# A chunked linear attention and two expert layers on one core: state products in four quadrants, weights converted in whole chunks, the second block's first product in halves, fewer loads up front

## The chip, the cores and the metric

The kernel runs on one core of a Trainium2 chip. The metric is the device time of one execution in microseconds, as the median of several runs; a separate profiled execution gives the trace. TensorE is called PE here, VectorE DVE, ScalarE ACT, GpSimd POOL, and SP is the engine whose queue issues the transfers.

## The reference

Attention with a decaying state runs over batch 4, 8 heads, 768 positions and head size 48. Its output, 3072 tokens of 384, goes through two expert layers, 384 to 2048 to 384 each.

```python
for t in range(S):
    kt, vt, rt = (k[:, :, t], v[:, :, t], r[:, :, t])
    cur = np.einsum('bhd,bhe->bhde', u[None] * kt, vt)
    y[:, :, t] = np.einsum('bhd,bhde->bhe', rt, state + cur)
    state = w[None, :, :, None] * state + np.einsum('bhd,bhe->bhde', kt, vt)
...
h = x @ w_in                                  # first layer
sp = np.where(h > 20.0, h, np.log1p(np.exp(np.minimum(h, 20.0))))
x = (h * np.tanh(sp)) @ w_out
...
h = np.maximum(x @ w_in, 0.0)                 # second layer
out = (h * h) @ w_out
```

The expert weights arrive as 64-bit floats and are turned into 32-bit ones on the core.

## The kernel before

**Work.** The positions are cut in 6 chunks of 128, so there are 24 attention units n = 4c + b (chunk c, batch b). A unit makes the scores of all heads (`scores`, tiles sc, L402), fills and masks a matrix A (`fill` on ACT, `select` on DVE), and sums the unit's y of two kinds of products: old state times r, one 112x112 product for each pair of heads (L433, only for c > 0), and A times v, one product for each head into 48 or 64 columns of the array (L442). Then it makes the new state's addend s (`s_pe`, L460), copies y to the stage tile yst (`y_out`, L473), and updates the state S. A pair of heads lies in rows 0 to 47 and 64 to 111.

The experts run over 12 blocks of 512 tokens, named in `BLOCKS` as (layer, chunk): (1,0), (1,1), (2,0), (2,1), (1,2) and so on. A block has 16 steps j, each over 128 of the 2048 hidden columns: `up` writes h (three 128x512 products), `act1` or `act2` makes g of it on ACT and DVE, and `down1` or `down2`, four steps later, adds to three or four accumulators acc. h has three buffers: up has two and flex one. The first two blocks are called full: their products are plain 32-bit ones on the tile wf (L575, L651). All other blocks split each operand into a high and a low half of a faster type and make three products for one, in `mm3` (L560 to L562).

**Weights.** Each step's weights are two halves of 384 columns. `conv_half` loads one half (raw, 64-bit), and turns it into wf with one ACT and three DVE instructions. The first layer's 16 chunks are converted while block 0 runs, the second's while blocks 1 and 2 run (`make_w2`, which also splits them in halves); both go to DRAM (wd1, wd2) and come back later.

**The spread.** After the four units of a chunk, six small transfers (`spread`) move the rows of the fourth pair of heads in yst between partitions, and `split_x` makes the expert input x of it.

**What sets the order.** Every instruction group is an item with an engine, an estimated time, and a due number. `Plan.order` plays all engines through once and writes the groups out in the order in which they would run; each engine then runs its own list strictly in that order, and SP's list is the queue of transfers. A ring of n buffers lets a tile start when the users of the n-th tile before it are done. `gates` hold a transfer back until a given `up` has been placed.

Of the kernel before, what the change touches and what calls it, by code (L numbers as in the profile page):

```python
# [33 lines left out]
class Tl:  # L34


    def __init__(self, ring, shape, dtype, name, ap=None):
        self.ring, self.shape, self.dtype, self.name, self.ap = ring, list(shape), dtype, name, ap
        self.users, self.writer, self.readers = [], None, []

    def get(self):
        if self.ap is None:
# [20 lines left out]
class Plan:  # L63
# [8 lines left out]
    def add(self, eng, dur, due, fn, r=(), w=(), deps=()):  # L72

        it = dict(n=len(self.items), eng=eng, dur=dur, due=due, fn=fn, deps=list(deps), after=[], ready=0.0)
# [16 lines left out]
    def order(self, rings):  # L91
        items = self.items
        for ring in rings:
            for k, t in enumerate(ring.tiles):
                if k >= ring.bufs:
                    t.users[0]["deps"] += ring.tiles[k - ring.bufs].users
                if k:
                    t.users[0]["after"].append(ring.tiles[k - 1].users[0])
# [14 lines left out]
        while events:  # L113
# [5 lines left out]
            for e, q in queue.items():  # L119
# [8 lines left out]
                else:  # L128
                    it["end"] = free[e] = now + it["dur"]
# [24 lines left out]
def rwkv_moe_kernel(ctx: ExitStack, tc: tile.TileContext, good, rk, nat, wT, wrow, ub, cst, w1, w2, out):  # L154
# [19 lines left out]
    for p, tag, bufs in (  # L174
        (w_p, "hi", NF + 1), (w_p, "lo", NF),
        (conv_p, "raw", 4), (conv_p, "wf", 2),
        (st_p, "stage", 1),
        (in_p, "r", 2), (in_p, "k", 2), (in_p, "nat", 2), (in_p, "v", 2),
        (a_p, "dg", 2), (a_p, "A", 2),
        (f_p, "e", 3), (f_p, "r", 2), (f_p, "ghi", 3), (f_p, "glo", 3), (f_p, "o", 3),  # L180
# [19 lines left out]
    def dma(o, i):  # L200
        nc.sync.dma_start(out=o, in_=i)
# [8 lines left out]
    one = const.tile([128, 1], F32, name="one")  # L210
    mask = cst_sb[:, 0:128].bitcast(I32)
# [5 lines left out]
    Sb = [fixed(const.tile([HP, NP, HP], F32, name=f"S{b}"), f"S{b}") for b in range(B)]  # L217
# [36 lines left out]
    for b in range(B):  # L254
        add("POOL", 0.5, -198 + b, lambda b=b: nc.gpsimd.memset(Sb[b].ap, 0.0), w=[Sb[b]])
# [16 lines left out]
    W = {}  # L272
    wd = {(2, x): fixed(dram_p.tile([NF, 128, 768], F32, name=f"wd2{x}"), f"wd2{x}") for x in ("hi", "lo")}
    wd1 = fixed(dram_p.tile([NF, 128, 768], F32, name="wd1"), "wd1")
    wdj = {}

    def conv_half(layer, j, half, f, fcol, due, raw_ring):
# [3 lines left out]
        raw = R[raw_ring].new([128, DM, 2], U32, f"raw{layer}_{j}_{half}")  # L281
        src = (w1, w2)[layer - 1][j, half]

        def load():
            dma(raw.get().rearrange("p d t -> p (d t)"), src.bitcast(U32))

        def fu():
            return f[:, fcol:fcol + DM].bitcast(U32)

        def s0():  # L290
            nc.scalar.activation(f[:, fcol:fcol + DM], raw[:, :, 1].bitcast(F32), AF.Copy, scale=HSC)
# [13 lines left out]
        add("ACT", 0.54, due - 1.5, s0, r=[raw], w=[f])  # L305
        add("DVE", 0.32, due - 1, s2, r=[f], w=[f])
        add("DVE", 0.53, due - 0.8, s3, r=[raw, f], w=[f])
        add("DVE", 0.53, due - 0.6, s4, r=[raw, f], w=[f])

    def split_w(layer, j, f, fcol, due):  # L310

        half = fcol // DM
        if half == 0 or (layer, j) not in W:
            W[layer, j] = [R[x].new([128, 768], F32R, f"w{x}{layer}_{j}") for x in ("hi", "lo")]
        hi, lo = W[layer, j]
        return hi, lo

    def split_hi(f, src, hi, dst):
        nc.scalar.activation(hi.get()[:, dst:dst + DM], f[:, src:src + DM], AF.Copy)

    def split_lo(f, src, hi, lo, dst):
        nc.vector.tensor_tensor(
            lo.get()[:, dst:dst + DM], f[:, src:src + DM], f32v(hi[:, dst:dst + DM]), ALU.subtract
        )

    def store_w(layer, j, due):
        for x, t in zip(("hi", "lo"), W[layer, j]):
            d = wdj[layer, j, x] = fixed(wd[layer, x].ap[j], f"wd{layer}{x}{j}")
            add("SP", 0.393, due, lambda d=d, t=t: dma(d.ap, f32v(t.ap)), r=[t], w=[d])

    def load_w(layer, j, due):
        W[layer, j] = [R[x].new([128, 768], F32R, f"w{x}{layer}_{j}r") for x in ("hi", "lo")]
        for x, t in zip(("hi", "lo"), W[layer, j]):
            d = wdj[layer, j, x]
# [8 lines left out]
    def load_unit(n, due):  # L343
        c, b = units[n]
        early = 2 <= n < B
        u = U[n] = {}
        shapes = ((HP, NP, C), (HP, NP, C), (128, 2, H, D), (128, H, D))
        for x, shape, src, mb in zip(
            ("r", "k", "nat", "v"), shapes, (rk[n, :, 0], rk[n, :, 1], nat[n, :, 0:2], nat[n, :, 2]),
            (0.229, 0.229, 0.393, 0.197),  # L350
        ):
            t = u[x] = R["hi" if early else x].new(shape, F32, f"{x}{n}")
# [4 lines left out]
    def rk_scale(n, x, due):  # L357
        t = U[n][x]
        add("DVE", 0.69, due, lambda: nc.vector.tensor_tensor(t.ap, t.ap, E, ALU.mult), r=[t, T_E], w=[t])
# [31 lines left out]
    def scores(n, due):  # L391
# [4 lines left out]
        def f():  # L396
            for e in range(2):
                ps[e].get()
            for p in range(NP):
                for e in range(2):  # L400
                    q = slice(64 * e, 64 * e + D)
                    nc.tensor.matmul(ps[e][:, p, :], u["k"][q, p, :], u["r"][q, p, :], start=True, stop=True)  # L402

        add("PE", 1.0, due, f, r=[u["k"], u["r"]], w=ps)
# [18 lines left out]

    def y_pe(n, due):
        u = U[n]
        c, b = units[n]
        ps = u["y"] = R["at"].new([128, NP, 128], F32, f"y{n}")

        def f():
            o = ps.get()  # L430
# [6 lines left out]
            v = u["v"].ap.rearrange("q h d -> q (h d)")  # L437
            for p in range(NP):
                for e in range(2):

                    h, m = 2 * p + e, 64 if not c and e == 0 else D
                    nc.tensor.matmul(  # L442
                        o[64 * e:64 * e + m, p, :], v[:, h * D:h * D + m], u["A", e][:, p, :],
# [3 lines left out]
        add("PE", 2.0 if c else 1.1, due, f, r=[u["r"], u["v"], u["A", 0], u["A", 1], Sb[b]], w=[ps])  # L447

    def s_pe(n, due):
# [3 lines left out]
        ps = u["s"] = R["at"].new([128, NP, 128], F32, f"s{n}")  # L453

        def f():
            o = ps.get()
            for p in range(NP):
                for e in range(2):
                    h = 2 * p + e
                    nc.tensor.matmul(  # L460
                        o[64 * e:64 * e + D, p, 0:D], u["nat"][:, 1, h, :], u["v"][:, h, :], start=True, stop=True
                    )

        add("PE", 0.6, due, f, r=[u["nat"], u["v"]], w=[ps])

    def y_out(n, due):
# [5 lines left out]
        def f():  # L472
            nc.scalar.activation(ys.get()[0:HP, :, b * C:(b + 1) * C], y[0:HP], AF.Copy)  # L473

        add("ACT", 0.6, due, f, r=[y], w=[ys])

    def state(n, due):
# [3 lines left out]
        ps = U[n]["s"]  # L481
        s = Sb[b]
        if c:
            add(
                "DVE", 0.6, due - 0.3,
# [547 lines left out]
```

## Time and profile before

| | us |
|---|---|
| median of 3 runs | 962.73 (961.9 to 962.97) |
| the profiled execution | 960.92 |
| its span in the trace | 959.0 |
| PE busy | 927.3 |
| DVE busy | 621.3 |
| ACT busy | 614.0 |

The span is the stretch that the trace covers; the execution's time is 1.9 us longer. Busy times overlap, since the engines run side by side. PE's first expert product starts 40.73 us after the span's start and its last product 951.77 us after it.

### The profile page before, as it was taken

To read this page: it belongs to the slowest core of one execution; us is meant where nothing else is said; L and a number is where in the kernel's file an instruction comes from. 1 tells how busy PE (TensorE), PEld (TensorE's weight loads), DVE (VectorE), ACT (ScalarE), POOL (GpSimd) and SP (SyncE) were. 2 spreads that over 40 slices of the span, in tenths; PEclk is the share of its full clock that TensorE was granted. 3 is DMA by queue.
4 is the path that set the end of the run, shared out by engine and by line. 5 is a ranking of instruction groups with operands and counts; after the bars stand their busy time and mean duration, and the time that the engine had idled before them with its cause. 6 is when DMAs were issued, how large, how long until landed. Compare 5 with 4: busy or idle time off the path is not lost.

```text
span 959.0 us, 13135 instructions
## 1 busy us (share of the span) xinstructions
PE 927.3 (97%) x4808; PEld 730.5 (76%) x4808; DVE 621.3 (65%) x1107; ACT 614.0 (64%) x1135; POOL 1.9 (0%) x9
## 2 busy tenths in 40 slices
PE   4699999999999999999999999999999999999997
PEld 3445444446988998888888889898888888899996
DVE  6899988999844566877988532363778877211211
ACT  3676567777755676787867655476767777544442
POOL 0000000000000000000000000000000000000000
PEclk9799999999999999999999999999999999999999
DMA  9894143578623443201366312243100065200001
GB/s 278 284 346 142 66 141 107 179 247 276 219 85 102 135 133 112 84 1 53 105 214 224 109 45 93 76 136 116 59 1 10 20 211 189 92 1 1 33 1 37
DMA packets 48106, 114.18 MB, mean 119 GB/s; under 512 B 5985, under 2 KB 12386, under 8 KB 48034
## 3 DMA queue, kind: packets, MB, share of 16 engines
q1 hardware_dynamic: 48034, 113.26, 35.9%
q8 instruction: 40, 0.66, 0.3%
q14 instruction: 32, 0.26, 0.1%
HBM read 88.47 MB, written 23.59 MB: 117 GB/s over the span
## 4 chain that ended last, share of the span: by engine, by line
PE 92%; DMA 4%; DVE 2%; issue 0%; SPq 0%; ACT 0%; DVEq 0%
PE h L560 12%; PE h L562 12%; PE h L561 11%; PE acc L651 8%; PE h L575 7%; PE acc L689 7%; PE acc L691 7%; PE acc L690 7%; PE acc L560 5%; PE acc L562 5%; PE acc L561 5%; PE sc L402 2%; PE y L442 2%; PE y L433 2%; DMA raw<-in_w_dram 1%; DMA r<-in_rk_dram 1%
## 5 line engine op out<-in xcount | busy, mean ns | idle before, releaser
L628 DVE TENSOR_TENSOR glo<-g,ghi 128x512 fp32r<-128x512 f32 x96 | 66.1, 689 | 150.4 <-ACT ghi L623 150.3
L636 ACT ACTIVATE e<-h 128x512 f32<-128x512 f32 x96 | 57.4, 598 | 116.4 <-PE h L562 116.2
L607 ACT ACTIVATE e<-h 128x512 f32<-128x512 f32 x96 | 56.9, 593 | 65.1 <-PE h L562 35.1
L623 ACT ACTIVATE ghi<-e 128x512 fp32r<-128x512 f32 x96 | 60.5, 630 | 59.1 <-PE acc L690 57.1
L575 PE MATMUL h<-x,wf 128*128 128x512 f32 x192 | 89.5, 605 | 4.9 <-ACT x L542 4.0
L651 PE MATMUL acc<-g,wf 128*128 128x512 f32 x192 | 88.1, 595 | 1.6 <-DVE g L604 1.6
L612 DVE TENSOR_TENSOR e<-e,r 128x512 f32<-128x512 f32 x96 | 66.1, 689 | 27.3 <-ACT r L611 27.0
L560 PE MATMUL acc<-ghi,whi 128*128 128x512 f32 x192 | 76.8, 400 | 0.0
L560 PE MATMUL h<-xh_a,whi 128*128 128x512 f32 x192 | 76.3, 397 | 0.0
L562 PE MATMUL h<-xh_a,wlo 128*128 128x512 f32 x192 | 75.6, 394 | 0.0
L562 PE MATMUL acc<-ghi,wlo 128*128 128x512 f32 x192 | 75.3, 392 | 0.0
L561 PE MATMUL h<-xl_a,whi 128*128 128x512 f32 x192 | 74.9, 390 | 0.0
L561 PE MATMUL acc<-glo,whi 128*128 128x512 f32 x192 | 74.8, 389 | 0.0
L575 PEld LDWEIGHTS h<-x,wf 128*128 128x128 f32 x192 | 36.6, 193 | 49.9 <-issue 39.9
L608 ACT ACTIVATE e<-e,one 128x512 f32<-128x512 f32 x96 | 69.4, 723 | 2.9
L651 PEld LDWEIGHTS acc<-g,wf 128*128 128x128 f32 x192 | 36.0, 190 | 44.7 <-issue 40.4
L601 DVE SCALAR_TENSOR_TENSOR r<-e,r 128x512 f32<-128x512 f32 x96 | 66.4, 692 | 3.2
L610 ACT ACTIVATE r<-e 128x512 f32<-128x512 f32 x96 | 59.7, 622 | 12.8 <-DVE e L598 12.5
L387 ACT ACTIVATE A<-cst_sb,dg 128x128 f32<-128x128 f32 x192 | 59.4, 388 | 6.2 <-DVE dg L372 6.2
L637 ACT ACTIVATE g<-e 128x512 f32<-128x512 f32 x96 | 60.6, 632 | 3.6 <-DVE glo L628 0.8
L611 ACT ACTIVATE r<-r 128x512 f32<-128x512 f32 x96 | 60.6, 632 | 2.9
L740 DVE TENSOR_TENSOR wlo<-wk,whi 128x768 fp32r<-128x768 f32 x32 | 30.6, 957 | 46.9 <-ACT g L637 21.1
(273 smaller groups left out, 2094.5 us busy)
## 6 DMA issues: line engine op xcount, KB each, us to landing
raw<-in_w_dram SPq DMA_DIRECT2D x64, 384.0 KB, 5.6
wk<-wd SPq DMA_DIRECT2D x32, 384.0 KB, 4.2
nat<-in_nat_dram SPq DMA_DIRECT2D x24, 384.0 KB, 4.1
wd<-wf SPq DMA_DIRECT2D x16, 384.0 KB, 3.1
wd2hi<-whi SPq DMA_DIRECT2D x16, 384.0 KB, 2.6
wd2lo<-wlo SPq DMA_DIRECT2D x16, 384.0 KB, 2.7
r<-in_rk_dram SPq DMA_DIRECT2D x24, 224.0 KB, 3.0
k<-in_rk_dram SPq DMA_DIRECT2D x24, 224.0 KB, 3.6
```

Of the source, the lines that this page charges most:

```text
L560: nc.tensor.matmul(o, wh, xh, start=first, stop=False, skip_group_check=True)
L561: nc.tensor.matmul(o, wh, xl, start=False, stop=False, skip_group_check=True)
L562: nc.tensor.matmul(o, wl, xh, start=False, stop=last, skip_group_check=True)
L575: nc.tensor.matmul(o, w[:, k * 128:(k + 1) * 128], xs[k][0].ap, start=(k == 0), stop=(k == 2))
L601: nc.vector.scalar_tensor_tensor(r.ap, e.ap, 2.0, r.ap, ALU.subtract, ALU.mult)
L608: add("ACT", 0.73, d + 0.2, lambda: nc.scalar.activation(e.ap, e.ap, AF.Square, bias=one), r=[e, T_one], w=[e])
L612: add("DVE", 0.69, d + 1, lambda: nc.vector.tensor_tensor(e.ap, e.ap, r.ap, ALU.mult), r=[e, r], w=[e])
L628: lambda: nc.vector.tensor_tensor(lo.get(), g.ap, f32v(hi.ap), ALU.subtract), r=[g, hi], w=[lo],
L651: nc.tensor.matmul(o, w[:, sl], hi.ap, start=(j == 0), stop=(j == NF - 1), skip_group_check=True)
L689: nc.tensor.matmul(o, hi[:, sl], wh[:, 384:768], start=(j == 0), stop=False, skip_group_check=True)
L690: nc.tensor.matmul(o, hi[:, sl], wl[:, 384:768], start=False, stop=False, skip_group_check=True)
L691: nc.tensor.matmul(o, lo[:, sl], wh[:, 384:768], start=False, stop=(j == NF - 1), skip_group_check=True)
```

## The change

1. The old-state products go from one 112x112 product for a pair of heads to one product for each head, in a 64x64 quarter of the array (`side` and `place` say which; pairs 1 and 2 swap their column halves). y of pairs 0 and 3 is in one PSUM bank and y of pairs 1 and 2 in another; s is written into the same two banks behind y. The state tile has 48 columns for each pair and not 112, and the updates of S and the copies of y go by bank.
2. A weight chunk is loaded and converted whole (768 columns). Two whole raw buffers take the place of four half ones.
3. Block 1's `up` uses halves: `FULL_UP` is (0,) and `FULL_DOWN` is (0, 1). The 384 up columns of each first-layer chunk are split (tiles wu), and x of chunk 1 too.
4. The first-layer chunks from the seventh on are loaded behind the first spread; r and k of a unit come in one transfer, and so do the two parts of nat with v. Half of the first spread is issued by ACT.
5. There are four output buffers o and not three.

```diff
-        (w_p, "hi", NF + 1), (w_p, "lo", NF),
-        (conv_p, "raw", 4), (conv_p, "wf", 2),
+        (w_p, "wa", NF // 2), (w_p, "wb", NF // 2),
+        (conv_p, "raw", 2), (conv_p, "wf", 2),
...
-        (f_p, "e", 3), (f_p, "r", 2), (f_p, "ghi", 3), (f_p, "glo", 3), (f_p, "o", 3),
+        (f_p, "e", 3), (f_p, "r", 2), (f_p, "ghi", 3), (f_p, "glo", 3), (f_p, "o", 4),
...
+    FULL_UP, FULL_DOWN = (0,), (0, 1)
...
-        raw = R[raw_ring].new([128, DM, 2], U32, f"raw{layer}_{j}_{half}")
+        raw = R[raw_ring].new([128, 768, 2], U32, f"raw{layer}_{j}")
...
-        it = add("SP", 0.393, due - 8 if layer == 2 else -175 + 10 * j, load, w=[raw])
+        it = add("SP", 0.786, load_due, load, w=[raw])
         if layer == 2:
-            gates.append((it, int(due - 8)))
+            gates.append((it, int(load_due)))
+        elif j >= 6:
+            gates.append((it, -1))
...
+    def side(p, e):
+        return 64 * (e ^ (p in (1, 2)))
+
+    def place(p):
+        return (0, 0) if p == 0 else (0, 1) if p == 3 else (1, p - 1)
...
             if c:
-                for p in range(NP):
+                for p, e in ((0, 0), (0, 1), (1, 1), (1, 0), (3, 0), (3, 1), (2, 1), (2, 0)):
+                    x, y = slice(64 * e, 64 * e + D), side(p, e)
+                    m = D if y else 64
                     nc.tensor.matmul(
-                        o[0:HP, p, :], Sb[b].ap[:, p, :], u["r"][:, p, :],
-                        start=(p == 0), stop=False, skip_group_check=True,
+                        out_y(p, y, m), Sb[b].ap[x, p * D:p * D + m], u["rk"][x, 0, p, :],
+                        start=(p < 2), stop=False, skip_group_check=True,
                     )
...
-        ps = u["s"] = R["at"].new([128, NP, 128], F32, f"s{n}")
+        ps = u["y"]
...
-        k_scale(n, t + d)
         for e in range(2):
             select(n, e, t + d)
         y_pe(n, t + 2 * d)
+        k_scale(n, t + d)
         s_pe(n, t + 2 * d)
...
-        def f():
+        def f(e):
+            eng = nc.scalar if c == 0 and e else nc.sync
             for k in range(3):
-                dma(ys[48:64, k, :], ys[16 * k:16 * k + 16, 3, :])
-                dma(ys[112:128, k, :], ys[64 + 16 * k:80 + 16 * k, 3, :])
+                dma(ys[64 * e + 48:64 * e + 64, k, :], ys[64 * e + 16 * k:64 * e + 16 * k + 16, 3, :], eng)
...
-        if blk in FULL:
+        if blk in FULL_UP:
             w = WF[j]
...
-        wh, wl = W[layer, j]
+        wh, wl = WU[j] if blk in FULL_DOWN else W[layer, j]
...
+            if 1 not in FULL_UP:
+                if j % 2 == 0:
+                    tile2 = R["wb"].new([128, 2, 2, 384], F32R, f"wu{j}")
+                WU[j] = [tile2.part(lambda ap, a=j % 2, x=x: ap[:, a, x]) for x in range(2)]
+                split_w(WF[j], slice(0, 384), *WU[j], NF + j - 3)
```

On PE the first place is unit 8, in block 2. Before, its y and s stand together (x4 and x8 are that many products, each of two passes):

```order
L562 MATMUL h_2186<-xh_b_1265,wlo_11_1907 128x512
L433 MATMUL y_2201<-r_1605,S_101 112x128 x4
L442 MATMUL y_2201<-A_0_1799,v_1620 48x128
L442 MATMUL y_2201<-A_1_1890,v_1620 48x128
...
L460 MATMUL s_2218<-v_1620,nat_1613 48x48 x8
L689 MATMUL acc_2_1862<-whi_8_1651,ghi_2112 128x384
```

Of the change (y_0 and y_1 are the two banks, and s has the name of y; L496 are the state products, L506 those of A, L525 those of s):

```order
L642 MATMUL h_2033<-xh_b_1172,w_11_1793 128x512
L496 MATMUL y_0_2048<-rk_1518,S_101 64x128
L496 MATMUL y_0_2048<-rk_1518,S_101 48x128
L496 MATMUL y_1_2051<-rk_1518,S_101 64x128
L496 MATMUL y_1_2051<-rk_1518,S_101 48x128
...
L506 MATMUL y_0_2048<-A_1_1846,nat_1522 48x128
L769 MATMUL acc_2_1737<-w_8_1628,ghi_1963 128x384
...
L771 MATMUL acc_2_1749<-w_8_1628,glo_1969 128x384
L525 MATMUL y_0_2048<-nat_1522 64x48
```

Four state products have become eight, and s has moved behind the twelve products of a `down2`. So it is in all of units 4 to 19; before, s stood right behind y in 11 of these 16.

The second place is ACT's list ahead of the first expert input x. Before, from the third unit's copy on:

```order
L473 ACTIVATE yst_292<-y_350 112x4x128
L387 ACTIVATE A_0_385<-cst_sb,dg_362 128x128 x4
L387 ACTIVATE A_1_393<-cst_sb,dg_362 128x128 x4
L497 ACTIVATE S_103<-s_364 48x4x48 x2
L291 ACTIVATE wf_0_192<-raw_0_1_150 128x384
L291 ACTIVATE wf_4_416<-raw_4_0_210 128x384
L291 ACTIVATE wf_1_243<-raw_1_1_162 128x384
L291 ACTIVATE wf_5_431<-raw_5_0_216 128x384
L473 ACTIVATE yst_292<-y_407 112x4x128
```

Of the change:

```order
L539 ACTIVATE yst_248<-y_1_322 112x2x128
L565 ACTIVATE S_103<-y_0_322 112x2x48
L565 ACTIVATE S_103<-y_1_322 112x96
L328 ACTIVATE wf_2_320<-raw_3_162 128x768
L328 ACTIVATE wf_4_373<-raw_4_164 128x768
L328 ACTIVATE wf_4_373<-raw_5_166 128x768
L539 ACTIVATE yst_248<-y_0_362 112x2x128
L539 ACTIVATE yst_248<-y_1_365 112x2x128
L219 DMA yst_248<-yst_248 16x512 x3
```

The copy of the fourth unit's y, on which the spread hangs, stands behind the conversion of the sixth weight chunk (raw_5) here, and behind the first half of that chunk before.

The third place is SP's queue around the first spread. Before, raw halves 6 to 8 went ahead of it, and then unit 4's r and k followed soon:

```order
L201 DMA raw_7_1_239<-in_w_dram 128x768
L201 DMA raw_8_0_398<-in_w_dram 128x768
L201 DMA yst_292<-yst_292 16x512 x6
L201 DMA raw_8_1_445<-in_w_dram 128x768
L201 DMA raw_9_0_450<-in_w_dram 128x768
L201 DMA r_454<-in_rk_dram 112x512
```

Of the change:

```order
L219 DMA raw_5_166<-in_w_dram 128x2x768
L219 DMA yst_248<-yst_248 16x512 x3
L219 DMA raw_6_397<-in_w_dram 128x2x768
L219 DMA raw_7_401<-in_w_dram 128x2x768
L219 DMA raw_8_403<-in_w_dram 128x2x768
L219 DMA raw_9_405<-in_w_dram 128x2x768
L219 DMA raw_10_408<-in_w_dram 128x2x768
L219 DMA rk_411<-in_rk_dram 112x1024
L219 DMA nat_413<-in_nat_dram 128x1152
```

Five whole chunks now stand between the spread and unit 4's r and k.

## Rows read from the trace of the kernel before

**Rows 1.** The page: busy us, share of the span, instructions.

```profile
PE 927.3 (97%) x4808; PEld 730.5 (76%) x4808; DVE 621.3 (65%) x1107; ACT 614.0 (64%) x1135; POOL 1.9 (0%) x9
```

**Rows 2.** Stretches: length, then each engine's busy us, granted clock, DMA share, GB/s.

```profile
0.00:10.00 10.00, 4.12 (x24) 3.56 (x24) 4.76 (x23) 1.28 (x1) 1.93 (x9) 1.00 0.74 229
10.00:20.00 10.00, 3.45 (x34) 2.95 (x36) 6.66 (x13) 5.30 (x16) 0.00 (x0) 1.00 1.05 318
20.00:30.00 10.00, 7.36 (x96) 6.32 (x96) 8.76 (x16) 6.06 (x19) 0.00 (x0) 0.83 1.04 348
120.00:140.00 20.00, 20.00 (x62) 8.91 (x61) 16.66 (x32) 12.40 (x22) 0.00 (x0) 1.00 0.43 149
240.00:400.00 160.00, 160.00 (x1025) 142.99 (x1025) 101.55 (x176) 104.60 (x202) 0.00 (x0) 1.00 0.40 130
```

**Rows 3.** Order of time, start-up: start, us, engine, line, operation [idle before <- releaser].

```profile
14.19 0.69 DVE L359 TENSOR_TENSOR k<-k,E 112x512 f32<-112x512 f32 x1 [1.94 <-DMA k<-in_rk_dram]
...
36.09 0.60 ACT L473 ACTIVATE yst<-y 112x512 f32<-112x512 f32 x1 [0.30 <-PE y L442]
36.71 3.77 SPq L201 DMA_DIRECT2D yst<-yst  x6
...
41.91 0.63 ACT L542 ACTIVATE x<-yst 128x512 f32<-128x512 f32 x1 [1.24 <-DMA yst<-yst]
...
45.80 0.60 ACT L607 ACTIVATE e<-h 128x512 f32<-128x512 f32 x1
...
46.43 0.72 ACT L608 ACTIVATE e<-e,one 128x512 f32<-128x512 f32 x1
...
49.56 0.42 DVE L598 TENSOR_SCALAR e<-e 128x512 f32<-128x512 f32 x1
...
55.46 0.69 DVE L604 SCALAR_TENSOR_TENSOR g<-r,h 128x512 f32<-128x512 f32 x1
```

**Rows 4.** The same view of PE, two waits in block 0.

```profile
56.20 2.84 PE L575 MATMUL h<-x,wf 128*128 128x512 f32 x6 [0.86 <-DVE g L604]
...
113.54 2.84 PE L651 MATMUL acc<-g,wf 128*128 128x512 f32 x6 [1.63 <-DVE g L604]
```

**Rows 5.** The chain that ended last, steady stretches: start, us to the next piece, what.

```profile
214.43 2.58 PE h L575 x6
...
219.58 0.23 PE h L560
...
270.24 0.88 PE y L433 x8
271.11 1.01 PE y L442 x16
272.12 0.36 PE s L460 x16
...
281.01 1.09 PE sc L402 x16
...
390.96 0.49 PE s L460 x16
391.46 0.43 PE acc L560
```

**Rows 6.** Groups by shape: count | busy us, mean ns of one | idle before.

```profile
L297 DVE SCALAR_TENSOR_TENSOR wf<-raw,wf 128x384 uint32<-128x384 uint32 x64 | 34.4, 555 | 0.9
L740 DVE TENSOR_TENSOR wlo<-wk,whi 128x768 fp32r<-128x768 f32 x32 | 30.6, 957 | 46.9 <-ACT g L637 21.1 <-issue 13.3 <-PE acc L690 8.6
L739 ACT ACTIVATE whi<-wk 128x768 fp32r<-128x768 f32 x32 | 26.6, 831 | 2.0 <-PE acc L691 1.5 <-DMA wk<-wd 0.5
L322 DVE TENSOR_TENSOR wlo<-wf,whi 128x384 fp32r<-128x384 f32 x32 | 17.5, 551 | 0.8 <-ACT whi L319 0.8
```

**Rows 7.** Order of time, the tail.

```profile
951.77 0.34 PE L691 MATMUL acc<-whi_15r,glo 128*128 128x384 f32 x1
953.05 0.56 DVE L702 TENSOR_SCALAR o<-acc 128x384 f32<-128x384 f32 x1 [1.40 <-DMA out_dram<-o]
```

More of the change, by code (lines that the diff above doesn't have):

```diff
@@ L94, in order @@
             for k, t in enumerate(ring.tiles):
[L95 to L98, printed above, removed]
+                for head in t.heads():
+                    if k >= ring.bufs:
+                        head["deps"] += ring.tiles[k - ring.bufs].everyone()
+                    if k:
+                        head["after"] += ring.tiles[k - 1].heads()
         left, succ, begun = {}, {}, {}
@@ L128, in order @@
                 else:
-                    it["end"] = free[e] = now + it["dur"]
+                    free[e] = now + it["dur"]
+                    it["end"] = free[e] + it["late"]
                 heapq.heappush(events, (free[e], -1))
@@ L310, in split_w @@
[L310 to L323, printed above, removed]
-        )
@@ new lines, in convert, with split_w @@
+        add("ACT", 0.87, due - 1.5, s0, r=[raw], w=[f])
+        add("DVE", 0.55, due - 1, s2, r=[f], w=[f])
+        add("DVE", 0.96, due - 0.8, s3, r=[raw, f], w=[f])
+        add("DVE", 0.96, due - 0.6, s4, r=[raw, f], w=[f])
+    def split_w(f, cols, hi, lo, due):
+        n = (cols.stop - cols.start) / 800
+        add("ACT", 0.1 + n, due, lambda: nc.scalar.activation(hi.get(), f.get()[:, cols], AF.Copy), r=[f], w=[hi])
+        add(
+            "DVE", 0.15 + n, due + 0.5,
+            lambda: nc.vector.tensor_tensor(lo.get(), f.get()[:, cols], f32v(hi.get()), ALU.subtract), r=[f, hi], w=[lo],
+        )
@@ L343, in load_unit @@
     def load_unit(n, due):
-        c, b = units[n]
         early = 2 <= n < B
         u = U[n] = {}
[L347 to L352, printed above, removed]
+        for x, shape, src, mb in (("rk", (HP, 2, NP, C), rk[n], 0.459), ("nat", (128, 3, H, D), nat[n], 0.59)):
+            t = u[x] = R["wa" if early else x].new(shape, F32, f"{x}{n}")
             it = add("SP", mb, due, lambda t=t, src=src: dma(t.get(), src), w=[t])
@@ L470, in y_out, with f @@
         ys, y = stage[c], U[n]["y"]
-        def f():
-            nc.scalar.activation(ys.get()[0:HP, :, b * C:(b + 1) * C], y[0:HP], AF.Copy)
-        add("ACT", 0.6, due, f, r=[y], w=[ys])
+        def f(i):
+            nc.scalar.activation(
+                ys.get()[0:HP, MINE[i], b * C:(b + 1) * C],
+                y[i][0:HP, 0:256].rearrange("q (p t) -> q p t", p=2), AF.Copy,
+            )
+        for i in range(2):
+            add("ACT", 0.38, due, partial(f, i), r=[y[i]], w=[ys])
     def state(n, due):
@@ L643, in down1 @@
         a = acc[blk]
-        w = WF[j] if blk in FULL else W[1, j]
+        full = blk in FULL_DOWN
+        w = (WF[j],) if full else W[1, j]
         def f():
+            ws_ = [t.get() for t in w]
             for m in range(3):
@@ L685, in f @@
         def f():
+            h_, l_ = (t.get()[:, 384:768] for t in (wh, wl))
             for m in range(B):
@@ L995, in _pack @@
     for t in range(3):
-        rows += list(range(2 * t * D, 2 * t * D + D)) + list(range(6 * D + 16 * t, 6 * D + 16 * t + 16))
-        rows += list(range((2 * t + 1) * D, (2 * t + 2) * D)) + list(range(7 * D + 16 * t, 7 * D + 16 * t + 16))
+        for e in range(2):
+            h = 2 * t + (e ^ (t in (1, 2)))
+            rows += list(range(h * D, h * D + D)) + list(range((6 + e) * D + 16 * t, (6 + e) * D + 16 * t + 16))
     def wcat(w_in, w_out):
```

267 lines of the change are left out of this document (147 added, 120 removed).

## The prediction

> **What bounds the kernel now.** I read the page first: PE is busy for 927.3 us, 97% of the span [rows 1], so any forecast must say which PE work goes and where PE idles. The stretches come second: from 120 us on PE is busy in full, and DVE (16.66 of 20 us, then 101.55 of 160) and ACT have room, so there the end moves with the sum of PE's work alone. The first 40 us are different: PE is mostly idle, transfers run at 229 to 348 GB/s, and DVE is at 8.76 of 10 us from 20 us on [rows 2]. So the order of time for the start-up comes third, and shows what leads to the first expert products: the copy of the fourth y at 36.09, six spread transfers from 36.71, the last x at 41.91, the first g at 55.46 [rows 3]. PE waits for that g at 56.20 (its third up buffer is freed by it) and once more, 1.63 us, at 113.54; I find no later wait of PE [rows 4]. Fourth, the chain in its steady part gives PE's prices: the time from a piece's start to the next one's, with no idle in it [rows 5].
>
> **Prices of PE's pieces** [rows 5]. Three plain 32-bit products of 512 columns take 2.58 us; one product of `mm3` takes 0.23, so nine take 2.08. Eight passes of the old state product take 0.88, which is 0.109 each. The sixteen passes of A times v, in two column halves of the array, take 1.01: that is eight times 0.109 and 0.13 more, so the two halves run side by side, and entering the halved array costs 0.13. The scores, in two row halves, give 1.09 for sixteen passes. Coming back to the full array costs 0.43 where a product in a row takes 0.23: 0.20. The addend s takes 0.36 right behind y, but 0.49 where it stands alone, and then the 0.20 is paid a second time.
>
> **Part by part.**
>
> Block 1's `up` in halves: 16 steps, each 2.58 - 2.08 = 0.50 less: **-7.9** (the unrounded difference is 0.495). It adds on DVE and ACT one 384-column split for each step (0.551 us on DVE [rows 6]) and three splits of x. That is 16 x 0.551 + 3 x 0.69, about 11 us of DVE. Cover: DVE's slack in block 1 (3.3 of 20 us) isn't enough alone, but the second layer's conversions, due only in block 2, can slide into the stretch behind 240 us, where DVE is idle for 58 of 160 us [rows 2]. Whole chunks give some of it back: an operation on 768 columns takes 0.957 where two on 384 take 2 x 0.555, so two of a chunk's three steps save 0.15 each [rows 6], about 10 us over 32 chunks. If the cover failed, those 11 us would be on the path.
>
> State products in quadrants, 20 units: before 0.88. Row halves and column halves each run at full pace side by side, so I take the four quarters to do so too: two products for each quarter are four passes, 4 x 0.109 + 0.13 to enter = 0.57. The entry of y behind it stays at 0.13, since it changes from quarters to halves in place of full to halves. 20 x (0.57 - 0.88) = **-6.2**. Bounds: -8.8 (no entry cost), and +2.5 if only two run at once, as in every row of the trace (8 x 0.109 + 0.13 = 1.00).
>
> s apart from y: in 11 more units, each 0.49 - 0.36 + 0.20 = 0.33: **+3.7**. It is the same price for each, from the row of a unit where that is so already. Bounds 0 (if the pieces overlap at these borders) and 3.7.
>
> Start-up. Six whole chunks and four units are ahead of the first spread: 9.30 MB (4 units of 0.459 + 0.590, chunks of 0.786, 0.385 of constants). The first three stretches carry 2.29, 3.18 and 3.48 MB, so all of it has passed by 31 us [rows 2]. A landing came 3.0 us behind that count for k of the second unit: 2.68 MB stood in the queue up to it, which had passed at 11.2, and its reader started at 14.19 [rows 3]. So chunk 6 lands at 34.0. ACT has its conversion (0.83, [rows 6]) ahead of the copy of the fourth y, so the copy ends at 35.6, and not at 36.69. The last x followed the issue of the six transfers by 5.20 us [rows 3]; three issues on each of two queues save half of the 3.77 us of issuing. The last x starts at 35.6 + 5.2 - 1.9 = 38.9, 3.0 earlier. From there to the first g: 3.9 to its exponential (45.80 - 41.91), 1.3 for that and the square (0.60 + 0.72), 0.4 for a step of DVE, 2.1 for a conversion (0.83) and two more steps of ACT (0.6 each, like the exponential), 2.1 for three steps of DVE (0.69 each): 48.7, say 49.3 with the passing on between engines. It is so early because unit 4's DVE work and fills, which stand between 46.43 and 55.46 in the rows [rows 3], now come behind it. At the first g PE has then done three `up` (7.7 us); before, it had done those and unit 4's sc, y and s (11.5 us). -6.9 + 3.8 = **-3.0**. Bounds: 0, if landing lags by 6 us and not 3; -5.7, if the sixth chunk is in before the fourth unit is done.
>
> Behind the spread. Unit 4's r and k now wait for five more chunks: 4.4 MB from 37 us at some 0.33 MB/us is 50.5, and 3 for the landing, 53.5; PE wants its scores at 54.7 (49.3 + 2.8 for the fourth `up` and 2.6 for the first `down1`), and DVE needs 1.2 between. nat, and the fill that depends on it, are as close. I put **+1.5** for this (0 to +5): what waits behind unit 4's scores on PE is the fifth `up` and all after it.
>
> The wait at 113.54 [rows 4]: that g was late because DVE was full, and up to there DVE's list is lighter by the whole-chunk operations, while PE's work up to there stays as it was. So I let it go: **-1.6** (bounds -1.6 and 0).
>
> Tail: the fourth o waited for the first one's transfer, since there were three buffers; it started at 953.05, where its products ended at about 952.1 [rows 7]: **-0.95**.
>
> At nothing: the loads of a unit in fewer transfers, the copies of y and the state updates by bank (ACT and DVE work behind 120 us, where both have room). If that cover went, two copies of 0.36 for one of 0.60 [rows 3] would cost 0.1 for each unit.
>
> Sum: -7.9 - 6.2 + 3.7 - 3.0 + 1.5 - 1.6 - 0.95 = -14.5 against the profiled 960.92, which gives 946.5. The median of the runs before is 962.73, 1.8 above the profiled execution; the forecast for the median is 962.7 - 14.5 = **948**.
>
> **Rivals.**
>
> A. The quarters run two at a time. Two quarters of different rows, (0,0) and (64,64), write the same PSUM bank, while in the scores each row half has a bank of its own; no row shows two row halves in one bank. If such a pair can't overlap, a group costs 1.00, the term is +2.5 and not -6.2, and the time is 957. For it: every row has two side by side at most. Against: both kinds of halves run at full pace. The Trainium skill (TensorEngine Tiling (Array Packing), Gotcha 1: PSUM Pressure) says that different row tiles cannot access the same PSUM bank at the same time; no run shown here has that. By that rule the time is 957.
>
> B. The start isn't won and block 0 waits. ACT's list is strict: chunk 6 ahead of the fourth copy, chunk 8 ahead of the first g's later steps, unit 4 behind five chunks. If landings lag by 6 us, the -3.0 is 0 and the +1.5 is +5: 954.5. For it: from 10 to 30 us the transfers' share stands at 1.05 and 1.04, so their engines have nothing left [rows 2]. Against: up to the last chunk that ACT needs for the fourth copy the queue holds 9.3 MB, and it held 8.9 before.
>
> C. Slower: the quarters run one after another. Sixteen passes at 0.109 and 0.13 are 1.87, 1.0 more than before; over 20 units +20 in place of -6.2, and the time is 975. It decides from a group of 1.3 us on (14.5 / 20 + 0.57). Against it stands that sixteen passes in halves take 1.01.
>
> D. The `up` term is hidden by DVE: block 1 becomes DVE's, and the 11 us of added splits come back: 959. For it: DVE is at 0.83 in 120 to 140 us and gets more [rows 2]. Against: in a step of 4.65 us only g (2.5, which is 0.42 and three times 0.69 [rows 3]) and the split (0.55) are due; the rest may slide.
>
> **How the numbers follow.** The forecast, 942 to 953 by its bounds, has 0.66; A 0.13; B 0.10; D 0.06; C 0.05. For the range I go from 940 (the better ends of the start and the quarters) to 957, which takes in A and B and leaves out C, D and some of the lower end. About 0.2% (2 us) is what a measurement of this kernel can tell from no change. All but C and part of D are faster by more: faster 0.92, within 0.2% 0.04, slower 0.04.
>
> **What would show it.** Block 1: nine products of 0.23 and three plain ones in turn, a step of 4.65. A quadrant group of eight products: 0.57 right, 1.00 is A, 1.9 is C. s alone at 0.49 and 0.20 behind it in every unit. The last x at 39, the first g at 49, and no wait of PE above 1 us from then on; a wait of PE at unit 4's scores is B, waits of `down1` for g around 150 to 200 us are D. The last o right behind the last product. The prediction is wrong if PE's idle time behind 60 us grows by more than 5 us, or a group costs more than 1.3.

## The result, and the profile after

The changed kernel takes 950.46 us (median of 4 runs, 949.64 to 952.96), and the kernel before takes 962.32 us beside it: the ratio is 0.9881, with a 95% interval of 0.9861 to 0.9901. So it is 11.9 us faster, where 14.5 were forecast (to 948); the time lies in the range. A second series of the changed kernel gave 950.56 us. The profiled execution took 949.64 us, 11.28 less than that of before, and its span is 947.9 us.

The page, in the columns of [rows 1]:

```profile
PE 920.5 (97%) x5016; PEld 729.2 (77%) x5016; DVE 609.2 (64%) x989; ACT 615.2 (65%) x1128; POOL 0.5 (0%) x9
```

Stretches, in the columns of [rows 2]:

```profile
20.00:30.00 10.00, 8.24 (x98) 7.36 (x96) 9.37 (x15) 9.03 (x28) 0.00 (x0) 1.00 0.99 383
30.00:40.00 10.00, 4.86 (x35) 3.01 (x36) 9.73 (x14) 5.66 (x14) 0.00 (x0) 0.58 0.35 99
120.00:140.00 20.00, 20.00 (x55) 10.08 (x54) 18.99 (x34) 15.82 (x28) 0.00 (x0) 1.00 0.50 168
240.00:400.00 160.00, 160.00 (x1076) 137.59 (x1076) 96.12 (x154) 103.24 (x196) 0.00 (x0) 1.00 0.36 118
```

PE is still full from 120 us on. DVE now stands at 18.99 of 20 us there, and not at 16.66: the added splits are in it. From 20 to 30 us transfers run at 383 GB/s, and between 30 and 40 us at 99, since what was let go up front has passed.

The order of time in the start-up (lines between are left out):

```profile
32.59 0.92 ACT L328 ACTIVATE wf<-raw 128x768 f32<-128x768 f32 x1 [0.16 <-DMA raw<-in_w_dram]
32.74 1.09 PE L525 MATMUL y<-nat 128*64 128x48 f32 x16 [0.62 <-DVE nat L467]
...
33.88 0.66 ACT L539 ACTIVATE yst<-y 112x256 f32<-112x256 f32 x2 [0.37 <-PE y L525]
34.29 1.87 SPq L219 DMA_DIRECT2D yst<-yst  x3
...
36.93 0.63 ACT L621 ACTIVATE x<-yst 128x512 f32<-128x512 f32 x1
...
37.61 10.06 PE L655 MATMUL h<-x,wf 128*128 128x512 f32 x18 [3.78 <-ACT x L621]
...
38.38 0.42 DVE L617 COPY x<-yst 128x512 f32<-128x512 f32 x1
...
47.45 0.69 DVE L684 SCALAR_TENSOR_TENSOR g<-r,h 128x512 f32<-128x512 f32 x1
...
53.05 1.23 DVE L404 TENSOR_TENSOR rk<-rk,E 112x1024 f32<-112x1024 f32 x1 [1.65 <-DMA rk<-in_rk_dram]
...
54.38 1.16 PE L449 MATMUL sc<-rk 48*128 48x128 f32 x16 [0.77 <-DVE rk L404]
...
57.41 2.84 PE L655 MATMUL h<-x,wf 128*128 128x512 f32 x6 [1.87 <-DVE g L684]
```

The first expert product starts at 37.61 (before: 40.73), and the first g at 47.45 (before: 55.46 [rows 3]). The copy of the fourth y starts at 33.88, and it waited for s (L525): s is written into the banks of y now, so the copy of y has to wait for it. Then unit 4's r and k land late, and PE stands twice: 0.77 us at unit 4's scores, and 1.87 us at the g behind them, since DVE did unit 4's four operations first.

Later in block 0 PE waits for g once more, near the place of the second wait in [rows 4]. It is 0.22 us now:

```profile
110.76 1.55 PE L655 MATMUL h<-x,wf 128*128 128x512 f32 x3 [0.22 <-DVE g L684]
```

The chain in steady stretches, in the columns of [rows 5]; the first four lines are the down and the first product of up in two steps of block 1, the others the pieces of one unit:

```profile
178.10 2.57 PE acc L733 x6
180.68 0.23 PE h L640
...
182.76 2.57 PE acc L733 x6
185.33 0.23 PE h L640
...
304.53 0.59 PE y L496 x14
305.12 1.02 PE y L506 x15
306.13 0.37 PE acc L769
...
308.43 0.59 PE y L525 x14
309.02 0.43 PE h L640
```

A step of block 1 is 182.76 - 178.10 = 4.66 us. The quadrant group takes 0.59 where the old products took 0.88. But s, which stands alone in all of units 4 to 19, takes 0.59 and not the 0.49 of the s that stood alone before.

The products of A behind them (L506) take 1.02, and took 1.01 behind the old ones, so going from quarters to halves costs no more than going from the full array to halves.

The tail, in the columns of [rows 7]:

```profile
940.86 0.33 PE L771 MATMUL acc<-w_15r,glo 128*128 128x384 f32 x1
941.23 0.56 DVE L782 TENSOR_SCALAR o<-acc 128x384 f32<-128x384 f32 x1 [0.49 <-PE acc L771]
```

The last o starts 0.37 us behind the start of the last product, where it was 1.28 before [rows 7]. But the end of the span is 947.9 - 940.86 = 7.0 us behind that product, and it was 959.0 - 951.77 = 7.2: from profile to profile only 0.2 of the 0.9 us reached the end. How much of it the change is worth, one profile can't say: in the twelve profiled executions of this study with four output buffers the last o starts 0.37 us behind the last product each time, and the end still comes between 6.3 and 7.3 us behind that product.

### The profile page after: what moved, and what is told of

Read it like the earlier page. It is cut to its first block, busy times and chain, and to the rows that moved or that the text cites. A ratio compares the mean times of both kernels' runs of the same rounds, so it can differ in the third digit from the quotient of the medians.

```text
span 947.9 us, 13265 instructions
## 1 busy us (share of the span) xinstructions
PE 920.5 (97%) x5016; PEld 729.2 (77%) x5016; DVE 609.2 (64%) x989; ACT 615.2 (65%) x1128; POOL 0.5 (0%) x9
## 4 chain that ended last, share of the span: by engine, by line
PE 92%; DMA 4%; DVE 2%; ACT 1%; SPq 0%; issue 0%; ACTq 0%
PE h L640 13%; PE h L642 13%; PE h L641 13%; PE acc L733 8%; PE acc L769 7%; PE acc L771 7%; PE acc L770 7%; PE acc L640 5%; PE acc L642 5%; PE acc L641 5%; PE h L655 3%; PE y L506 2%; PE sc L449 2%; DMA raw<-in_w_dram 2%; DMA nat<-in_nat_dram 2%; PE y L496 1%
## 5 line engine op out<-in xcount | busy, mean ns | idle before, releaser
L703 ACT ACTIVATE ghi<-e 128x512 fp32r<-128x512 f32 x96 | 60.4, 629 | 56.1 <-PE acc L770 56.1
L640 PE MATMUL acc<-ghi,w 128*128 128x512 f32 x192 | 76.9, 401 | 0.0
L640 PE MATMUL h<-xh_a,w 128*128 128x512 f32 x192 | 76.6, 399 | 0.0
L642 PE MATMUL h<-xh_a,w 128*128 128x512 f32 x192 | 75.7, 394 | 0.0
L642 PE MATMUL acc<-ghi,w 128*128 128x512 f32 x192 | 75.3, 392 | 0.0
L641 PE MATMUL h<-xl_a,w 128*128 128x512 f32 x192 | 74.9, 390 | 0.0
L641 PE MATMUL acc<-glo,w 128*128 128x512 f32 x192 | 74.7, 389 | 0.0
L708 DVE TENSOR_TENSOR glo<-e,ghi 128x512 fp32r<-128x512 f32 x64 | 44.1, 689 | 18.5 <-ACT ghi L705 14.7
L655 PE MATMUL h<-x,wf 128*128 128x512 f32 x96 | 46.5, 625 | 6.4 <-ACT x L621 3.8
L705 ACT ACTIVATE ghi<-e 128x512 fp32r<-128x512 f32 x64 | 40.1, 626 | 18.8 <-DVE e L684 18.4
```

The costliest lines, as they stand in the source:

```text
L640: nc.tensor.matmul(o, wh, xh, start=first, stop=False, skip_group_check=True)
L641: nc.tensor.matmul(o, wh, xl, start=False, stop=False, skip_group_check=True)
L642: nc.tensor.matmul(o, wl, xh, start=False, stop=last, skip_group_check=True)
L655: nc.tensor.matmul(o, a[:, k * 128:(k + 1) * 128], xs[k][0].ap, start=(k == 0), stop=(k == 2))
L708: lambda: nc.vector.tensor_tensor(lo.get(), g.ap, f32v(hi.ap), ALU.subtract), r=[g, hi], w=[lo],
```

## The experiments

Each is the changed kernel with one edit, unless said otherwise; ratios are to the kernel before, as above (the changed kernel: 0.9881).

### Block 1's up in plain products again

```diff
-    FULL_UP, FULL_DOWN = (0,), (0, 1)
+    FULL_UP, FULL_DOWN = (0, 1), (0, 1)
```

> Block 1's up in plain 32-bit products again (with it go its splits); all else as changed. Theory: TensorE is the bound in block 1, and 16 steps go from 4.66 back to 5.16 us: 7.9 us more, about 958.4. Rival: VectorE, which is busy for 19 of 20 us in block 1 with the added splits, had taken part of the gain back (waits or conversions that finish late): only 4 to 6 us more, 954.5 to 956.5.

Measured: 958.1 us, ratio 0.9958 (0.9945 to 0.9971), 7.6 us more. The theory holds. The chain of this run in block 1:

```profile
182.10 2.58 PE h L655 x6
184.67 2.58 PE acc L733 x6
187.25 2.58 PE h L655 x6
```

So a step is 187.25 - 182.10 = 5.15 us, and the changed one 4.66: 16 x 0.49 is 7.9 us. Its profiled execution (959.53 us) lost some more at another place: between 58 and 60 us PE's granted clock was 0.50, the lower of its two levels (1.2 and 2.4 GHz). Just before, PE had waited for unit 4's r and k and then for the g behind unit 4's DVE work (0.95 and 1.63 us). The `up` at 57.24 took 4.54 us there, and 2.84 elsewhere. The stretches, in the columns of [rows 2]:

```profile
56.00:58.00 2.00, 0.76 (x2) 0.40 (x3) 1.97 (x5) 1.38 (x5) 0.00 (x0) 0.91 1.02 396
58.00:60.00 2.00, 2.00 (x4) 0.91 (x3) 2.00 (x4) 1.97 (x6) 0.00 (x0) 0.50 1.03 401
```

That DVE is busy for 68.2 of 72.5 us from block 1's first `up` to its last (133.66 to 206.20) costs PE nothing there: the changed kernel has no wait of PE behind 111 us.

### s of 48 columns

The even heads' s takes 64 weight columns in the change (the rows 48 to 63 of its bank are filled with it), the odd ones' 48. With 48 for all, the state is added by row half.

```diff
-                    h, m = 2 * p + e, D if e else 64
+                    h, m = 2 * p + e, D if e or units[n][0] else 64
...
-        for i in range(2):
-            add("DVE" if c else "ACT", 0.27, due, partial(f, i), r=[ps[i], s], w=[s])
+        for i in range(2):
+            for q in (slice(0, D), slice(64, HP)) if c else (slice(0, HP),):
+                add("DVE" if c else "ACT", 0.27, due, partial(f, i, q), r=[ps[i], s], w=[s])
```

> s in 48 weight columns for every head, in units 4 to 19 (in the changed kernel the even heads take 64), and the state is added by row half, four additions for each unit in place of two. Theory: a pass of s takes as long as its weights have columns (0.058 us at 64, 0.045 at 48, both read from the changed kernel's trace), so s alone falls from 0.59 to 0.49 us and the time by 16 x 0.10 = 1.6 us, to about 949. Rival: the longer s comes from its place in the two banks of y, or from standing between other pieces: it stays at 0.59 and the time at 950.5.

Measured: 956.09 us, ratio 0.9929 (0.9906 to 0.9951): 5.6 us slower, which neither theory had. Yet s alone takes what the theory said:

```profile
288.56 0.49 PE y L525 x16
289.05 0.43 PE h L641
```

What it lost is elsewhere: the plan, with two more DVE items for each unit, wrote another order in blocks 0 and 1, and PE waited there for g, 2.10 us at 111.32 and 2.28 us at 214.18. Behind the second wait PE's granted clock was at its lower level as well (0.50 from 216 to 218 us). So the same edit was made with the two additions inside the old item, which leaves every group in its place:

```diff
         def f(i):
-            o = states(b)[:, MINE[i]]
-            a = ps[i][0:HP, 256:256 + 2 * D].rearrange("q (p d) -> q p d", p=2)
+            for q in (slice(0, D), slice(64, HP)) if c else (slice(0, HP),):
+                o = states(b)[q, MINE[i]]
+                a = ps[i][q, 256:256 + 2 * D].rearrange("q (p d) -> q p d", p=2)
```

> s in 48 weight columns in units 4 to 19 once more, with every instruction group at its old place: the two additions by row half stand inside the item that was one addition. Theory: the loss of the first try came from the order that the planner made of more and longer VectorE items (two waits for g, 2.10 and 2.28 us, that the changed kernel does not have), and not from s, which took 0.49; now 16 x 0.10 = 1.6 us less, about 949. Rival: the two more additions in each unit make g late by themselves on a VectorE that is full in blocks 0 and 1: the two waits come again, and the time is 953 to 956.

Measured: 951.1 us (947.3 to 952.15), ratio 0.9881 (0.9863 to 0.9898). The large loss is gone, so it came from the order; the wait of 2.28 us is not there, and of the one of 2.10 us, 0.99 are left. But the 1.6 us don't show in the times, whose runs lie 5 us apart. In the trace s takes 0.49, and from the end of the fifth up of block 2 to that of the first up of block 7 PE needs 362.6 us in place of 363.8, with 12 units in between: 0.10 for each. The price is shown; whether the time falls by it is not.

### s right behind y

```diff
+        if n >= B:
+            k_scale(n, t + d)
         y_pe(n, t + 2 * d)
-        k_scale(n, t + d)
-        s_pe(n, t + 2 * d)
+        if n < B:
+            k_scale(n, t + d)
+            s_pe(n, t + 2 * d)
```

and `y_pe` ends with the products of s for 0 < c < 5.

> s right behind y again in units 4 to 19, as one piece of TensorE, with the scaling of k ahead of y. Theory: the second entry and the second return go; a unit's y, s and returns take 0.59 + 1.02 + 0.47 + 0.20 = 2.28 in place of 2.59, so 16 x 0.31 = 5.0 us less, about 945.5. Rival: y now waits for the scaling of k on VectorE, which is busy for 19 of 20 us in block 0 and in block 1; TensorE then waits in front of y, and of the 5 us little is left (above 949).

Measured: 946.06 us, ratio 0.9832 (0.9817 to 0.9847), 4.4 us less, close to the 5.0 of the theory. The pieces of one unit:

```profile
257.51 0.59 PE y L496 x14
258.10 1.02 PE y L506 x15
259.12 0.45 PE y L529 x15
259.57 0.37 PE acc L774
```

From the group's start to the first full product behind it are 2.06 us, and the return is paid once. In the changed kernel y's pieces take 1.60 and s 0.59, and two returns are paid. PE doesn't wait more for it: behind its first expert product it stands for 2.50 us in all, and in the changed kernel for 3.38.

### Unit 4's loads first

```diff
-            it = add("SP", mb, due, lambda t=t, src=src: dma(t.get(), src), w=[t])
+            it = add("SP", mb, -135 if n == B else due, lambda t=t, src=src: dma(t.get(), src), w=[t])
```

> The loads of unit 4 (r with k, and nat) are the first ones behind the spread, ahead of five weight chunks in place of behind them. Theory: the waits of 0.77 us (scores of unit 4) and 1.87 us (the g behind unit 4's VectorE work) go, 2.6 us less, about 948. Rival: the weight chunks land 3 us later and VectorE is full in that stretch, so the same waits turn up one or two steps later: 950 to 951.

Measured: 947.65 us, ratio 0.985 (0.9836 to 0.9863), 2.8 us less, as the theory said. r and k are there at 39.82 and the scores run at 41.23, without a wait of PE:

```profile
39.82 1.22 DVE L404 TENSOR_TENSOR rk<-rk,E 112x1024 f32<-112x1024 f32 x1 [1.41 <-DMA rk<-in_rk_dram]
...
41.23 0.94 PE L449 MATMUL sc<-rk 48*128 48x128 f32 x12
```

The rival has a part in it: a wait of 1.35 us for g stands at 107.80 now, and one of 0.82 us at unit 4's s (50.17). Behind the first expert product PE stands for 2.18 us in all, and in the changed kernel for 3.38, so the waits account for 1.2 us of the 2.8. In the profiled execution the first product also came 1.28 us sooner (36.33), which the edit can't have done, since all up to the spread is the same. How much of the 2.8 us is the edit's is not settled beyond the 1.2.

### The copies of unit 3's y ahead of its s

```diff
+        if n == B - 1:
+            y_out(n, t + 2.5 * d)
         s_pe(n, t + 2 * d)
-        y_out(n, t + 2.5 * d)
+        if n != B - 1:
+            y_out(n, t + 2.5 * d)
```

> In unit 3 alone the two copies of y stand ahead of s (s is written into the same two banks, and the copies wait for it). Theory: the spread starts when y is there, at about 32.3 in place of 33.9, and the first expert product follows: 1.6 us less, about 949. Rival: the first products then wait for the first g, which hangs on VectorE's conversions of weights in that stretch, and the time stays within 0.5 us of 950.5.

Measured: 947.42 us, ratio 0.9851 (0.9838 to 0.9864): 3.0 us less, more than the theory said. The copies start at 31.97:

```profile
31.97 0.63 ACT L539 ACTIVATE yst<-y 112x256 f32<-112x256 f32 x2
32.35 1.88 SPq L219 DMA_DIRECT2D yst<-yst  x3
32.49 0.58 PEld L525 LDWEIGHTS y<-nat 128*64 128x64 f32 x16 [1.14 <-ACT yst L539]
```

In this plan the conversion of raw_5 stands behind the copies, and one of the five chunks goes behind unit 4's loads, so that their waits of 0.77 and 1.87 us are gone too; the wait of 1.35 us for g in block 0 stands here as well (107.44). Which part of the 3.0 us belongs to the copies alone was not taken apart.

### Three more chunks ahead of the spread

```diff
-        elif j >= 6:
+        elif j >= 9:
```

> Three more weight chunks (the seventh to the ninth) are let go ahead of the first spread, which is about what the kernel before had there. Theory: it is the empty queue that makes the spread quick (2.6 us from its issue to the first x, against 3.4 before, and 3.6 to the last of the ACT ones against 5.2), so the first product comes 1 to 3 us later, 951.5 to 953.5. Rival: the three chunks land while the copies are made, the spread is no slower, and what VectorE gets earlier makes up for it: 950 to 951.

Measured: 949.79 us, ratio 0.9868 (0.985 to 0.9886): no difference that shows. Both are half right. The copy of the fourth y starts as in the changed kernel (34.23), but from the issue of the spread to the first x are 5.8 us (40.48 - 34.64), where they were 2.6, and the first product comes at 41.15:

```profile
34.64 2.15 SPq L219 DMA_DIRECT2D yst<-yst  x3
...
40.48 1.14 ACT L621 ACTIVATE x<-yst 128x512 f32<-128x512 f32 x2
...
44.99 1.23 DVE L404 TENSOR_TENSOR rk<-rk,E 112x1024 f32<-112x1024 f32 x1 [0.63 <-DMA rk<-in_rk_dram]
```

What else moved at that time shows in the stretch from 32 to 36 us, first in the changed kernel, then in this one (columns as in [rows 2]):

```profile
32.00:36.00 4.00, 1.21 (x17) 0.93 (x16) 3.93 (x7) 2.01 (x4) 0.00 (x0) 0.50 0.07 15
```

```profile
32.00:36.00 4.00, 1.34 (x28) 0.96 (x23) 3.90 (x6) 2.48 (x5) 0.00 (x0) 1.00 0.99 380
```

The time from the issue of the six transfers to their landing, least, median and most, in the same order:

```profile
DMA to landing us min/median/max: 1.9/2.0/2.3
DMA to landing us min/median/max: 4.6/4.9/5.4
```

So the empty queue does make the spread quick: 15 GB/s around it, and not 380. (The first x stands behind a chunk's conversion in ACT's list here, which started at 39.67 and took 0.91 us, so the 5.8 us is not the spread's alone.) But one chunk alone is left between the spread and unit 4's loads; its r and k come 8 us sooner, and behind the first product PE waits for 1.15 us in all, not 3.38. A start that is 3.5 us later costs nothing that shows at the end.

### The order of the quarters

```diff
-                for p, e in ((0, 0), (0, 1), (1, 1), (1, 0), (3, 0), (3, 1), (2, 1), (2, 0)):
+                for p, e in ((0, 0), (1, 0), (3, 0), (2, 0), (0, 1), (1, 1), (3, 1), (2, 1)):
```

> The eight state products of a unit in another order: the four of the array's upper row half first, then the four of the lower one; the same quarters, banks and additions otherwise. Theory: TensorE issues in order, and a product waits only for the one before it in its own quarter, so now two quarters run at a time and a group takes 1.00 us (8 x 0.109 + 0.13) in place of 0.59: 20 x 0.41 = 8.2 us more, about 958.7. Rival: the order doesn't matter, since each quarter has its own queue: 0.59 again and 950.5.

Measured: 951.94 us, ratio 0.99 (0.9883 to 0.9916), which can't be told from the changed kernel's 0.9884 beside it. The theory falls: the group takes 0.61, and its first passes in all four quarters start within 0.04 us.

```profile
303.21 0.61 PE y L496 x15
303.82 1.02 PE y L506 x15
```

So a quarter's products don't hold up those of another quarter that are issued behind them; the order of these eight doesn't matter.

### Three output buffers

```diff
-        (f_p, "o", 4),
+        (f_p, "o", 3),
```

> Three output buffers o in place of four. Theory: the end of the kernel comes 0.2 us later and no more, since in the changed kernel the last o started 0.9 us sooner after the last product, but the span ended only 0.2 us sooner after it (7.04 in place of 7.23): 950.7. Rival: the whole 0.95 us comes back: 951.4. Both are under what the times can tell; the trace's distance from the last product to the end tells them apart.

Measured: 949.39 us, ratio 0.988 (0.9863 to 0.9896), the same. In the trace the last o starts 1.51 us behind the last product:

```profile
938.48 0.34 PE L771 MATMUL acc<-w_15r,glo 128*128 128x384 f32 x1
939.99 0.56 DVE L782 TENSOR_SCALAR o<-acc 128x384 f32<-128x384 f32 x1 [1.64 <-DMA out_dram<-o]
```

Its span ends at 945.9, 7.4 us behind that product, where the changed kernel needs 7.0. The fourth buffer brings the o 1.1 us forward. What it brings the end isn't settled by these two traces, whose 0.4 us lies within the 6.3 to 7.3 us of the twelve executions with four buffers. Their mean is 6.9, and the two executions with three (before and this one) have 7.2 and 7.4, so some 0.4 us of the 0.95 seem to reach the end. The plan moved some other groups as well, so the time is not the buffers' alone.

### The three edits together

They are s of 48 columns right behind y (with the two additions inside the old item), unit 4's loads first, and the copies of unit 3 first; each is as above.

> Together: s of 48 columns right behind y in units 4 to 19, unit 4's loads ahead of the five chunks, the copies of unit 3's y ahead of its s. Theory: the parts add up where they lie apart: 4.4 (s behind y) and 1.4 (16 x 0.09, s at 0.36) in the stretch where TensorE is full, and 2.8 to 3.0 for the start, where the last two shorten the same waits: about 942. Rival: with less work on TensorE in block 0 the waits for g on a full VectorE take 2 us or more of it back: 944 or above.

Measured: 941.82 us (940.58 to 942.95), ratio 0.9787 (0.977 to 0.9804): 20.5 us faster than the kernel before, and 8.6 faster than the change. This is the best version of the study, and the sum of the theory (942) arrives. s takes 0.36 behind y:

```profile
257.16 0.36 PE y L529 x16
```

The rival's time is not there, but its waits are, two for g in block 0, of 0.83 and 1.82 us. The second is not new in kind: 1.35 us stood near its place with each of the two start-up edits alone.

```profile
80.84 2.84 PE L664 MATMUL h<-x,wf 128*128 128x512 f32 x6 [0.83 <-DVE g L693]
106.98 2.84 PE L664 MATMUL h<-x,wf 128*128 128x512 f32 x6 [1.82 <-DVE g L693]
```

### The scaling of k on GpSimd

```diff
+            eng, dur, v = ("POOL", 1.2, nc.gpsimd) if units[n][0] == 1 else ("DVE", 0.56, nc.vector)
             add(
-                "DVE", 0.56, due,
-                lambda: nc.vector.tensor_tensor(t[:, 1], t[:, 1], EK
+                eng, dur, due,
+                lambda: v.tensor_tensor(t[:, 1], t[:, 1], EK
```

> The kernel with all three edits together, and in units 4 to 7 the scaling of k on GpSimd, which does nothing else then. Theory: VectorE is what makes g late in block 0 (waits of 0.83 and 1.82 us are left there in the kernel of the three edits); four operations of 0.55 us less on it take most of the two waits away: 939.5 to 940.5. Rival: GpSimd is slow at it or slows VectorE down, y waits for the scaling, and the time is 943 or above.

Measured: 941.92 us, ratio 0.9791 (0.9773 to 0.9809), the same as without it. GpSimd needs 998 ns for one of the four operations (DVE 550), no engine stood waiting for it, and the two waits stay, 0.95 and 1.89 us. So they don't hang on 0.55 us of DVE's work for each unit. Behind the second wait the profiled execution had PE's lower clock (0.50 from 110 to 112 us; the `up` there took 4.54 us and not 2.84), so its time alone would not tell; the waits do. Whether they hang on DVE's order or on its sum is left open.

### The changed kernel once more

> The changed kernel once more, on the chip of these runs. Theory: 950.5, as before; its first expert product comes at 36.5 to 38 us after the span's start, since in the runs whose start is the same program it came between 35.57 and 37.66.

Measured: 950.56 us, ratio 0.9884 (0.9867 to 0.9901). The time is as said, but its first product came at 39.17, outside what was expected:

```profile
39.17 3.78 PE L655 MATMUL h<-x,wf 128*128 128x512 f32 x4 [3.79 <-ACT x L621]
```

## Why the prediction was right, and where its sizes were off

The terms against what was measured, from one profiled execution to the other, in us (the last section says how far the start of one execution can be trusted):

| term | forecast | measured | from |
|---|---|---|---|
| block 1's up in halves | -7.9 | -7.9 | steps of 4.66 and 5.15; 7.6 in the times |
| state products in quadrants | -6.2 | -5.8 | 20 x (0.59 - 0.88) |
| s apart from y | +3.7 | +5.2 | 11 x (0.59 + 0.20 - 0.36) + 5 x (0.59 - 0.49) |
| start-up, to the first product | -3.0 | -3.1 | 37.61 for 40.73 |
| first g, waits of PE | in the above | -0.9 | 0.51 for 0.86 [rows 4] and 0.56 (unit 4's y, at 52.30 before) |
| unit 4 behind five chunks | +1.5 | +2.6 | 0.77 and 1.87 |
| the wait at 113.54 | -1.6 | -1.4 | 0.22 is left |
| tail | -0.95 | -0.2 | 7.0 for 7.2 |
| sum | -14.5 | -11.5 | the two executions: -11.28 |

**Block 1** went as worked out. The slack was smaller than the prediction read, since its row of 120 to 140 us is mostly block 0: before, block 1's first `up` starts at 137.02, and from there to the last one DVE has about 2 us of 20 left, not 3.3. So the rest had to slide, as the prediction said, and it did: the first split of the second layer's weights starts at 157.44 us, and at 146.77 in the run with plain products. Rival D is out, since PE does not wait there.

**The quadrants.** All four quarters run at once (0.59, forecast 0.57, and 1.00 if only two did), so rivals A and C are out. Two quarters of different rows that write different partitions of one bank did run side by side: (0,0) and (64,64) are both in the first bank of y. The Trainium skill (TensorEngine Tiling (Array Packing), Gotcha 1: PSUM Pressure) says that different row tiles cannot access the same PSUM bank at the same time; by that rule the group would have taken 1.00 and the time been 957. For two quarters with different output partitions the trace does not agree. For two that write the same partitions of one bank it wasn't tried, and the kernel keeps those in two banks.

**s** is the term that was mis-sized most. Its price of 0.49 was read from a row in which each pass loads 48 weight columns; in the change the even heads' s loads 64, which the rows of the order showed (64x48). The runs with 48 columns give 0.49 alone and 0.36 behind y, the changed kernel and the run with s behind y 0.59 and 0.45. So the difference of 0.10 is that of the columns. The forecast also left the 5 units where s stood alone already out of the count.

**Start-up.** The forecast of 3.0 stands against 3.1 to the first product and 0.9 of waits, 4.0 in all, and it came partly by another way than the prediction had it. The copy of the fourth y started 2.2 us sooner; it waited for s, with which it shares its banks since the change, and the prediction didn't see that. Nothing stood in the queue ahead of the spread (landing 2.0 us behind issue in the median, and 4.9 with three chunks more). But before the change it was as quick to land (2.0); what became quicker is the issue, 3.77 us for six on one queue and 1.87 and 2.15 for three on each of two, as the prediction had it. Of rival B the lost start did not come, and of its 5 us at unit 4 about half did. Part of what the start won was handed back: the chunks taken out of its way stand ahead of unit 4's r and k, and those cost 2.6 us, not 1.5 (2.0 to 2.6 in the eight profiled executions with all five chunks ahead of unit 4). That the two belong together is shown from both sides: with three chunks back up front the first product is 3.5 us later and the time the same, and with unit 4's loads first these two waits are gone and the time is 2.8 us less.

**Tail.** That an o starts 0.9 us sooner was right; that the whole of it reaches the end is not borne out, and how much does is not settled (0.2 here, some 0.4 over all profiled executions). What holds the end up behind the last o was not taken apart.

**Luck.** Five terms were too good for the change by some 4 us together (s 1.5, unit 4 1.1, the tail 0.8, the quadrants 0.4, the wait 0.2), and the start too bad by 1.0. That the forecast is off by 2.5 us in the median, and not by more, owes something to that, and to where the starts of the two profiled executions fell.

## What to carry to other kernels

Price an operation by a row of its own shape: sixteen passes of s cost 0.59 us with 64 weight columns in half of them and 0.49 with 48 in all. When loads are taken out of one critical transfer's way, ask who stands behind them now; here that was the next unit, and the order in which both are served is worth 2.8 us in the times (1.2 of them shown as waits of PE). And an edit under a planner is two edits, its own and the new order: put it inside an existing item first, so that nothing else moves (956.1 us with new items, 951.1 without).

## What was not expected of the hardware

- The start differs from one execution to the next. In nine executions whose instructions are the same up to the spread, the first expert product came between 35.36 and 39.17 us after the span's start, and between the two profiles of the changed kernel, where it came 1.56 us later (39.17 for 37.61), the last product came 1.30 us later (942.16 for 940.86). So the start alone can put two profiles some us apart, and the 3.1 us between the profiled starts of before and of the change are no better known than that. Where it comes from was not found; loads land at other times, and PE's granted clock from 32 to 36 us was 0.50 in four of these executions, 1.00 in one and between them in the rest.
- The four quarters don't wait for one another in the order of issue (0.59 and 0.61 in two orders).
- Six small transfers landed 2.0 us (median) behind their issue where 15 GB/s moved beside them, and 4.9 us beside the last of nine chunks at 380 GB/s.
